# Early loads of a frequency-filter and mixer kernel reordered: filters behind the stage-1 stores, weights behind the low-rank loads, low-rank loads in three parts; stage 1 of units 2 and 3 moved later

## The chip, the cores and the metric

The kernel runs on one core of a Trainium2 chip. The metric is device time in microseconds (us), the median of several runs. Engines are named as in the profile: PE is TensorE (matmuls), PEld its weight loads, DVE VectorE, ACT ScalarE, POOL GpSimd, SP SyncE. SPq, ACTq and POOLq are DMA issues by these engines. Runs of one and the same kernel spread by 1 to 1.5%, so a difference needs an interval; each ratio below is given with its 95% interval.

One caution for all single traces: the profiled run of the kernel before had a granted PE clock of only 0.70 over its first 70 us. The other traces had 0.85 to 0.96 there, but for e17 (0.70), with the same program in many of them. Where a trace is compared with that of the kernel before in this stretch, the clock differs too.

## The reference, cut to what matters

```python
X = np.fft.rfft(x, axis=1)                  # x: 8 batches, 3136 tokens, 256 channels
y = np.fft.irfft(X * (filt_r + 1j * filt_i), n=3136, axis=1)
h = y.transpose(0, 2, 1) @ U @ V            # low rank, 32
u = y + h.transpose(0, 2, 1)
out = u + np.maximum(u @ w_ch1, 0) @ w_ch2  # 256 -> 1024 -> 256
```

## The kernel before: the parts that matter

3136 is 64 x 49. The transform is done in two steps with matmuls, and back. The eight batches are five units: two of one batch (units 0 and 1), three of two (units 2 to 4). For each unit:

- stage 1 (`f1`): x is loaded by POOL (in tiles x[0], x[1] and so on; the small rest is `xl`), transformed, evicted (copied out of the matmul's accumulators) to `asb` (the rest to `al`), and stored to the DRAM scratch `ct1` (shown as ct_0 to ct_4, one name for both scratches of a unit);
- stage 2 (`mid`): `a2` is loaded from it, 32 steps k multiply it with `tf2`, with the filters `fab` (DVE writes `uv`; for later units `fab` has a second half, filled by two mirror copies of 784 KB each just after the low rank of unit 0) and with `g3`; the result `esb` is stored to the scratch `ct2`;
- low rank: `eh` and `eb` are loaded from `ct2`, `ph` is accumulated, and DVE writes the rank-32 part into `eb` (`put_h`);
- mixer: `ut`, then `phh` (w1, relu `h`; its first matmul is called the first mm1), then `pc` (w2), then the output store `och`.

The mixer of unit n runs while stages 1 and 2 and low rank of unit n+1 are dealt out between its matmuls by a plan of steps. A step is about 1 us of mixer work. `S[n]` is the step at which the mixer of unit n starts.

```python
def hold(dst, src):                    # a 1x1 copy into the tile to be loaded:
    nc.vector.tensor_copy(dst, src)    # the load must wait for it, and it waits for src
...
    def third_loads(src):              # called at k == 10 of stage 2 of unit 0
        hold(usb[0:1, 0:1], src)
        nc.gpsimd.dma_start(usb, ...); nc.gpsimd.dma_start(vnat[64:96, :], moe_V)
        nc.gpsimd.dma_start(w1sb, ...); nc.gpsimd.dma_start(w2sb, ...)
    def fourth_loads(src):             # called when the low-rank loads of unit 0 land
        for c in range(4):
            load_x(units[1], c, src)
...
    deal(f1s[1], 7, 4, 11)             # stage 1 of unit 1: seven calls, steps 4 to 11
    deal(mids[1], 33, 17, 33)
    deal_f1(units[2], 12, (0, 2, 6, 7))
    deal(mids[2], 33, 44, S[2] - 29)
...
    # in the main loop, five steps before stage 1 of unit 2: its first two x loads,
    # held until x[2] of unit 1 has landed
    load_x(x_step[step], c, units[1].x[2][0:1, 0, 0:1] if x_step[step].n == 2 else None)
```

## Time and profile before

635.51 us, median of the first three runs (630.59 to 636.77). The profiled run spans 629.3 us.

The page of the kernel before, first its busy times, then its slices. A digit is tenths of a slice of 15.7 us; PEclk is the granted clock of PE, DMA the mean share of the 16 DMA engines.

```profile
span 629.3 us, 10769 instructions
PE 552.8 (88%) x4350; PEld 388.0 (62%) x4350; DVE 330.0 (52%) x390; ACT 334.6 (53%) x623; POOL 41.7 (7%) x62
...
PE   3294576999699993989999999999999999999997
...
PEclk9558576999979997989999999999999999999999
DMA  9898979999835749868567787455433862331112
```

PE is full in nearly the whole second half. It is idle for 76.5 us (629.3 minus 552.8), nearly all of it in the first 280 us, and 4.6 us at the end.

The chain that ended last, of the kernel before; columns are start, length and what.

```profile
9.72 7.16 DMA ct_0<-asb
16.96 6.25 DMA ct_0<-al
23.25 4.47 DMA a_161<-ct_0
28.58 10.14 DMA g_78<-g
...
69.42 13.53 DMA x<-in_x_dram
...
94.31 3.48 ACTq L320
99.42 3.85 ACTq L320
...
159.70 9.85 DMA eh<-ct_1
...
230.67 10.60 DMA ct_3<-asb
241.27 7.31 DMA eh<-ct_2
```

The early chain goes from transfer to transfer. Two of its pieces were the targets of the change: the stores of stage 1 at 10 to 23 us, and the loads and stores around the low rank of unit 2.

The timeline of the kernel before around 83 us; the bracket is the idle time before the instruction and what ended it.

```profile
83.05 0.14 DVE L174 COPY x<-x 1x1 f16<-1x1 f16 x1 [9.28 <-DMA x<-in_x_dram]
83.12 1.20 DVE L539 CAST ut<-pu 128x1024 f16<-128x1024 f32 x1
83.74 0.57 POOL L167 DMA_DIRECT2D x<-in_x_dram  x1 [12.32 <-DVE x L174]
84.38 1.01 PE L304 MATMUL pf<-x,wf_64 128*128 128x512 f16 x2 [3.87 <-DVE ut L539]
```

The first line is the hold for x of unit 2. It stands in the VectorE queue until x[2] of unit 1 lands at 83 us. The eviction of `ut` stands behind it, and PE stands 3.9 us behind that.

### The profile page before, as it was taken

The numbers are of one execution on the slowest core, as the hardware profiler recorded it, in microseconds if no ns is written. First come the engines' busy times: TensorE is split into PE (matmuls) and PEld (weight loads), VectorE is DVE, ScalarE is ACT, GpSimd is POOL, SyncE is SP. The second block draws the span as 40 slices with busy tenths as digits, with TensorE's granted clock in tenths as the row PEclk, the third lists the DMA queues.
The fourth block names the chain that finished last, engine by engine and source line by source line (L and its number), as shares of the span: only waits on it lengthen the run. The fifth ranks groups of instructions, "written<-read, shape, count | busy, mean of one in ns | idle before, by whom it ended". The sixth has DMA issues, their size and how long they took to land.

```text
span 629.3 us, 10769 instructions
## 1 busy us (share of the span) xinstructions
PE 552.8 (88%) x4350; PEld 388.0 (62%) x4350; DVE 330.0 (52%) x390; ACT 334.6 (53%) x623; POOL 41.7 (7%) x62
## 2 busy tenths in 40 slices
PE   3294576999699993989999999999999999999997
PEld 0183242767456661657766676777677767777776
DVE  5274222786278870263888743576866325333332
ACT  0043232667156662546667665665766655666663
POOL 3345110100000000000000000000000000000000
PEclk9558576999979997989999999999999999999999
DMA  9898979999835749868567787455433862331112
GB/s 176 230 205 193 214 183 236 246 250 244 244 119 161 216 81 286 208 166 227 171 187 173 208 245 249 156 148 187 120 131 119 239 202 83 99 100 67 66 67 102
DMA packets 68002, 110.18 MB, mean 175 GB/s; under 512 B 5549, under 2 KB 49438, under 8 KB 66604
## 3 DMA queue, kind: packets, MB, share of 16 engines
q1 hardware_dynamic: 36240, 81.17, 41.2%
q0 software_dynamic: 7312, 15.91, 15.8%
q10 hardware_dynamic: 24400, 12.41, 6.9%
q8 instruction: 34, 0.56, 0.4%
q14 instruction: 16, 0.13, 0.1%
HBM read 72.38 MB, written 51.38 MB: 197 GB/s over the span
## 4 chain that ended last, share of the span: by engine, by line
PE 73%; DMA 16%; issue 4%; DVE 3%; ACT 2%; ACTq 1%; POOL 0%; SPq 0%; POOLq 0%; DVEq 0%
PE phh L550 25%; PE pc L590 24%; PE pe L360 8%; PE pz L382 5%; PE pu L532 3%; PE pc L564 3%; DMA x<-in_x_dram 3%; PE pf L304 3%; DMA ct_3<-asb 2%; DMA g_78<-g 2%; DMA eh<-ct_1 2%; ACTq L320 1%; DMA eh<-ct_2 1%; DMA ct_0<-asb 1%; PE ph L476 1%
## 5 line engine op out<-in xcount | busy, mean ns | idle before, releaser
L550 PE MATMUL phh<-ut,w1sb 128*128 128x512 f16 (+2 forms) x848 | 251.7, 377 | 3.5 <-DVE ut L539 3.0
L397 DVE TENSOR_TENSOR uv<-pz,fab 98x1024 f16<-98x1024 f32 (+1 forms) x128 | 137.8, 1087 | 35.3 <-PE pz L382 34.8
L600 DVE COPY och<-pc 128x512 f32<-128x512 f32 x96 | 66.3, 690 | 165.8 <-PE pc L564 162.6
L550 PEld LDWEIGHTS <-w1sb 128*128 128x128 f16 x848 | 105.6, 146 | 36.7 <-issue 16.7
L366 ACT CAST esb<-pe 98x512 f16<-98x512 f32 (+1 forms) x160 | 79.5, 501 | 64.6 <-PE pe L360 57.0
L360 PE MATMUL pe<-uv,g_78 98*98 98x512 f16 (+1 forms) x320 | 85.7, 353 | 1.4 <-DMA g_78<-g 0.8
L539 DVE CAST ut<-pu 128x1024 f16<-128x1024 f32 (+1 forms) x51 | 59.9, 1174 | 21.6 <-PE pu L532 21.4
L564 PE MATMUL pc<-idn,ut 128*128 128x128 f16 x394 | 54.8, 220 | 0.0
L360 PEld LDWEIGHTS <-g_78 98*98 98x98 f16 x320 | 41.3, 132 | 19.4 <-issue 5.6
L564 PEld LDWEIGHTS <-ut 128*128 128x128 f16 x394 | 38.7, 98 | 6.7 <-issue 0.3
L382 PEld LDWEIGHTS <-tf_74 98*98 98x98 f16 x160 | 21.7, 136 | 20.2 <-DMA a_163<-ct_0 15.3
L304 PE MATMUL pf<-x,wf_64 128*128 128x512 f16 x84 | 27.9, 402 | 6.8 <-DVE ut L539 6.3
L476 PE MATMUL ph<-eh,ut_94 128*32 128x512 f16 (+1 forms) x120 | 10.7, 384 | 26.2 <-DMA eh<-ct_0 11.6
L167 POOL DMA_DIRECT2D x<-in_x_dram x24 | 14.1, 602 | 266.5 <-PE pf L304 225.1
L309 DVE CAST asb<-pf 128x1024 f16<-128x1024 f32 x21 | 25.6, 1219 | 11.5 <-PE pf L304 8.9
L307 ACT CAST asb<-pf 128x1024 f16<-128x1024 f32 x21 | 21.3, 1013 | 10.7 <-PE pf L304 6.7
L390 DVE TENSOR_TENSOR uv<-pz,fab 98x512 f16<-98x512 f32 x32 | 20.9, 687 | 5.1 <-PE pz L387 2.9
L476 PEld LDWEIGHTS <-ut_94 128*32 128x32 f16 x120 | 3.3, 97 | 31.6 <-issue 20.7
L366 ACT ACT_TABLE_LOAD x1 | 1.3, 1283 | 30.2 <-DVE uv L390 30.2
L382 PE MATMUL pz<-a_161,tf_74 98*98 98x256 f16 x8 | 3.2, 403 | 15.2 <-DMA a_163<-ct_0 14.9
L532 PEld LDWEIGHTS <-eb_97 96*128 96x128 f16 x256 | 10.3, 100 | 7.5 <-issue 4.7
L486 ACT CAST hp<-ph 128x512 f16<-128x512 f32 (+1 forms) x5 | 2.5, 501 | 23.1 <-PE ph L483 23.1
(1427 smaller groups left out, 1046.2 us busy)
## 6 DMA issues: line engine op xcount, KB each, us to landing
out_dram<-och SPq DMA_DIRECT2D x48, 512.0 KB
x<-in_x_dram POOLq DMA_DIRECT2D x24, 512.0 KB, 8.0
ct_2<-esb SPq DMA_DIRECT2D x16, 196.0 KB
ct_3<-esb SPq DMA_DIRECT2D x16, 196.0 KB
ct_4<-esb SPq DMA_DIRECT2D x16, 196.0 KB
ct_2<-asb ACTq DMA_DIRECT2D x6, 512.0 KB
ct_3<-asb ACTq DMA_DIRECT2D x6, 512.0 KB
eh<-ct_2 SPq DMA_DIRECT2D x6, 512.0 KB
```

The source lines that it names most:

```text
L304: nc.tensor.matmul(pf[:, i, :], wx, u.x[c][:, r:r + 2, :], start=True, stop=True)
L309: nc.vector.tensor_copy(dst, pf)
L360: nc.tensor.matmul(pe[0:98, 0:bd], g3[:, (2 * k + l) * 98:(2 * k + l + 1) * 98], uv[:, l * bd:(l + 1) * bd], start=(l == 0), stop=(l == 1))
L366: nc.scalar.copy(st["esb"][:, i, :], pe[0:98, 0:bd])
L382: nc.tensor.matmul(pz[0:98, 0:bd], wz, a2[c][:, i, :], start=True, stop=True)
L397: nc.vector.tensor_mul(uv.rearrange("p (f b d) -> p f b d", f=2, b=nb), zin, fin)
L532: nc.tensor.matmul(pu[:, dh, 64 * i:64 * i + 64], e2[0:96, d0:d0 + 128], sv[0:96, 64 * r:64 * r + 64], start=(i == 0), stop=True, skip_gro ...
L539: nc.vector.tensor_copy(gr.ut[:, :, 0:n].rearrange("p h (c q s) -> p h c q s", q=64, s=2), pu[:, :, 0:n].rearrange("p h (c s q) -> p h c q ...
L550: nc.tensor.matmul(ph[:, 0:n], w1v[:, dh, :, t], gr.ut[:, dh, 0:n], start=(dh == 0), stop=(dh == 1))
L564: nc.tensor.matmul(o[:, dh * 128:dh * 128 + 128], gr.ut[:, dh, t0:t0 + n], idn, start=False, stop=(dh == 1), skip_group_check=True)
L590: nc.tensor.matmul(o, gr.h[tt][:, i * 128:(i + 1) * 128], w2sb[:, tt * DM:(tt + 1) * DM], start=(tt == 0), stop=False, skip_group_check=True)
L600: nc.vector.tensor_copy(dst, gr.pc.rearrange("p (j d) -> p j d", j=2))
```

## The change

Its intent: let the stage-1 stores of unit 0, and later its low-rank loads, have the DMA engines to themselves, by moving loads that are wanted later; and keep stage 1 of units 2 and 3 away from the loads of the units ahead. The diff, cut to its core:

```diff
-    load_filters(PARTS[0], PARTS[1])                 # was right behind x of unit 0
+    def first_loads(src):                            # src: the last stage-1 eviction
+        hold(tf2[0:1, 0:1], src);  nc.sync.dma_start(tf2[:, 0:...], ...)
+        hold(g3[0:1, 0:1], src);   nc.scalar.dma_start(g3[:, 0:2 * KA], ...)
+        load_part(0, tf2[:, 0:1])                    # filters wait for tf2 to land
     def second_loads(src):                           # a2[0] has landed
-        for i in range(2, 4):
-            load_part(i, src)
+        load_part(1, src)                            # parts 2 and 3 at k == 1 and k == 6
     def third_loads(src):
-        nc.gpsimd.dma_start(w1sb, ...); nc.gpsimd.dma_start(w2sb, ...)
     def fourth_loads(src):
+        hold(w1sb[96:97, 0:1], src);  nc.gpsimd.dma_start(w1sb, ...)
+        hold(w2sb[96:97, 0:1], src);  nc.gpsimd.dma_start(w2sb, ...)
         for c in range(4):
             load_x(units[1], c, src)
@@ stage 1 of unit 0
-                        nc.vector.tensor_copy(dst[:, i, :], pf)
+                        (nc.scalar.copy if i else nc.vector.tensor_copy)(dst[:, i, :], pf)
@@ low rank of unit 0: rows 0 to 31, 32 to 63 -> 0 to 31, 32 to 47, 48 to 63
-            a = 32
+            for z in (32, 48):
...
-        if i == 24:                                  # i counts k of stage 2 of unit 0
+        if i in (22, 29):
             next(ranks[0])
@@ plan
-    deal(f1s[1], 7, 4, 11);  deal(mids[1], 33, 17, 33)
-    deal_f1(units[2], 12, ...);  deal(mids[2], 33, 44, S[2] - 29)
+    deal(f1s[1], 7, 5, 12);  deal(mids[1], 33, 18, 34)
+    deal_f1(units[2], 20, ...);  deal(mids[2], 33, 53, S[2] - 26)
-    deal_rank(units[1], 34, S[1] - 7);  deal_rank(units[2], S[2] - 28, S[2] - 7)
+    deal_rank(units[1], 35, S[1] - 6);  deal_rank(units[2], S[2] - 25, S[2] - 6)
@@ unit 3 (and one step of unit 4's low rank)
-        stage 1 from S[2] - 38, stage 2 from S[2] + 21 to S[3] - 36, low rank S[3] - 35 to S[3] - 8
+        stage 1 from S[2] - 18, stage 2 from S[2] + 40 to S[3] - 30, low rank S[3] - 29 to S[3] - 7
```

More of the change, by code (lines that the diff above doesn't have):

```diff
@@ L222, in load_part @@
     def load_part(i, src):
-        hold(fab[0:1, 0, PARTS[i], 0:1], src)
-        load_filters(PARTS[i], PARTS[i + 1])
+        a, z = PARTS[i], PARTS[i + 1]
+        hold(fab[:, 0, a, 0:1], src)
+        if z == NK:
+            hold(fab[:, 0, 31, 0:1], src)
+        load_filters(a, z)
+    def first_loads(src):
+        hold(tf2[0:1, 0:1], src)
+        nc.sync.dma_start(tf2[:, 0:PARTS[1] * 147], tf2_d[:, 0:PARTS[1] * 147])
+        hold(g3[0:1, 0:1], src)
+        nc.scalar.dma_start(g3[:, 0:2 * KA], g_d[:, 0:2 * KA])
+        load_part(0, tf2[:, 0:1])
     def second_loads(src):
-        for i in range(2, 4):
-            load_part(i, src)
+        load_part(1, src)
         for t, d in ((s2, s2_d), (s2t, s2t_d), (kr, kr_d)):
-            hold(t[0:1, 0:1], src)
+            hold(t[0:1, 0:1], src[0:1])
             nc.scalar.dma_start(t, d)
         ka = PARTS[1] * 147
-        hold(tf2[0:1, ka:ka + 1], src)
+        hold(tf2[0:1, ka:ka + 1], src[0:1])
         nc.sync.dma_start(tf2[:, ka:], tf2_d[:, ka:])
-        hold(g3[0:1, 2 * KA:2 * KA + 1], src)
+        hold(g3[0:1, 2 * KA:2 * KA + 1], src[0:1])
         nc.sync.dma_start(g3[:, 2 * KA:], g_d[:, 2 * KA:])
@@ L241, in third_loads, with fourth_loads @@
         nc.gpsimd.dma_start(vnat[64:96, :], moe_V)
+    def fourth_loads(src):
+        hold(w1sb[96:97, 0:1], src)
         nc.gpsimd.dma_start(w1sb, moe_w_ch1.rearrange("(h dd) c -> dd h c", h=2))
+        hold(w2sb[96:97, 0:1], src)
         nc.gpsimd.dma_start(w2sb, moe_w_ch2.rearrange("(cc t) e -> cc (t e)", t=8))
-    def fourth_loads(src):
         for c in range(4):
@@ L309, in f1 @@
                         nc.vector.tensor_copy(dst, pf)
-                if u.n == 0:
-                    if (c, half) == (1, 0):
-                        hold(tf2[0:1, 0:1], asb[0:1, 0, 0:1])
-                        nc.sync.dma_start(tf2[:, 0:PARTS[1] * 147], tf2_d[:, 0:PARTS[1] * 147])
-                    if (c, half) == (2, 0):
-                        hold(g3[0:1, 0:1], asb[0:1, 0, 0:1])
-                        nc.scalar.dma_start(g3[:, 0:2 * KA], g_d[:, 0:2 * KA])
                 if half and nb == 1:
@@ L331, in f1 @@
         al = sb.tile([m, DM], F16, tag="al", bufs=1)
-        if u.n == 0:
-            nc.vector.tensor_copy(al, pf[0:m, 0, 0:DM])
-            load_part(1, al[0:1, 0:1])
-        else:
-            nc.scalar.copy(al, pf[0:m, 0, 0:DM])
+        nc.scalar.copy(al, pf[0:m, 0, 0:DM])
         (nc.sync if u.n == 0 else nc.scalar).dma_start(
             dram(u.ct1, 48 * 64 * bd, [[DM, m], [1, DM]]), al)
+        if u.n == 0:
+            first_loads(al[0:1, 0:1])
         yield
@@ L374, in mid @@
         if u.n == 0:
-            second_loads(a2[0][0:1, 0, 0:1])
+            second_loads(a2[0][:, 0, 0:1])
         for k in range(NK):
@@ L397, in mid @@
                 nc.vector.tensor_mul(uv.rearrange("p (f b d) -> p f b d", f=2, b=nb), zin, fin)
+            if u.n == 0 and k in (1, 6):
+                load_part(2 if k == 1 else 3, uv[:, 0:1])
             if u.n == 0 and k == 10:
@@ L457, in low_rank @@
         if u.n == 0:
-            a = 32
-            for c in range(3):
-                load(c, 0, a)
-            load_l(0, a)
-            yield
+            for z in (32, 48):
+                for c in range(3):
+                    load(c, a, z)
+                load_l(a, z)
+                a = z
+                yield
         for c in range(3):
@@ L466, in low_rank @@
         load_l(a)
-        u.held = eh[2]
+        u.held = eh[1]
         u.ready = True
@@ L628 @@
             next(sr)
-        if i == 24:
+        if i in (22, 29):
             next(ranks[0])
-        if i == 28:
+        if i == 25:
             u_hat()
@@ L634 @@
     next(ranks[0])
-    fourth_loads(units[0].held[64:65, 0, 0:1])
+    fourth_loads(units[0].held[96:97, 0, 0:1])
     for _ in range(3):
@@ L659, in deal_f1 @@
             k += 1
-    deal(f1s[1], 7, 4, 11)
-    deal(mids[1], 33, 17, 33)
-    deal_f1(units[2], 12, (0, 2, 6, 7))
-    deal(mids[2], 33, 44, S[2] - 29)
+    deal(f1s[1], 7, 5, 12)
+    deal(mids[1], 33, 18, 34)
+    deal_f1(units[2], 20, (0, 2, 6, 7))
+    deal(mids[2], 33, 53, S[2] - 26)
     def deal_rank(u, a, z):
@@ L672, in deal_rank @@
         plan[step_at(z + 2)].append(ranks[u.n])
-    deal_rank(units[1], 34, S[1] - 7)
-    deal_rank(units[2], S[2] - 28, S[2] - 7)
+    deal_rank(units[1], 35, S[1] - 6)
+    deal_rank(units[2], S[2] - 25, S[2] - 6)
     for u in units[3:]:
-        deal_f1(u, S[u.n - 1] - (38 if u.n == 3 else 60), (1, 7))
-        deal(mids[u.n], 33, S[u.n - 1] + (21 if u.n == 3 else 3), S[u.n] - 36)
-        deal_rank(u, S[u.n] - 35, S[u.n] - 8)
+        deal_f1(u, S[u.n - 1] - (18 if u.n == 3 else 60), (1, 7))
+        deal(mids[u.n], 33, S[u.n - 1] + (40 if u.n == 3 else 3), S[u.n] - (30 if u.n == 3 else 36))
+        deal_rank(u, S[u.n] - (29 if u.n == 3 else 35), S[u.n] - 7)
     x_step = {max(0, next(i for i, p in enumerate(plan) if f1s[u.n] in p) - 5): u for u in units[2:]}
```

## The prediction

> **What bounds it now.** The page gives PE 552.8 us busy of 629.3 (88%). The table by stretches shows PE full from about 280 to 600 us; the change removes no PE work, so only idle time and lost clock can be won. The 76 us of PE idle lie at 0-30 us (23), 50-70 (13), 70-90 (6), 90-110 (6), 160-200 (7), 240-280 (11) and the end (5). In the first 140 us the DMA share is 0.7 to 1.1 in every 10 us, at about 216 GB/s: the start is bound by transfers, and PE is granted only 0.5 to 0.7 of its clock in much of it. The chain of waits names the ct_0 stores (7.2 us), the al store behind them (6.3), the a2 load (4.5), the g3 remainder (10.1), the low-rank loads, x of unit 1 (13.5), stage-1 stores of unit 1 (ACT blocked 3.5 and 3.9 us), later eh<-ct_1 (9.9) and, after ct_3<-asb (10.6), eh<-ct_2 (7.3; PE waits 10.5 us at 238-248).
>
> **What the change does.** It moves bytes and removes none. (a) 0-28 us: filter parts 0 and 1, tf2 and g3 (about 1.3 MB landed) no longer share the engines with 1.6 MB of stage-1 stores; ACT takes half of the evictions (0.68 us each on DVE, about 1 us won). Estimate: first uv at 25 to 26 us instead of 28.5; filter part 0 now waits for tf2 to land, which caps the gain. (b) w1 and w2 (1 MB landed, 7.5 and 9.9 us) leave 45-55 us, so the last esb stores (issued 55.5, landed 61.6) and the low-rank loads should land sooner, but w1 is then wanted some 8 us after its issue. Estimate: first mm1 at 66 us instead of 73.2. (c) A DVE hold for x of unit 2 waits for x[2] of unit 1 until 83.05 and blocks the ut eviction behind it: PE idle 3.9 us. Eight steps later it should find its data there. Unit 2's x and stores also leave the 84-110 us where ACT was blocked. Estimate: 5 to 7 us. (d) Stage 1 of unit 3 leaves the low-rank loads of unit 2 alone: most of the 10.5 us wait and part of the slow clock after it (0.83 in 240-280). Estimate: 8 us. (e) The eh<-ct_1 wait near 165 us: 1 to 2 us at most; stage 1 of unit 2 now overlaps it more.
>
> The Trainium skill, "DMA: Bandwidth & Descriptors" (Queues, rings and completion order), says each DMA engine goes round-robin between the queues with work; so a load issued early takes its share from the stores of the moment. The 6.3 us for a 32 KB store agree.
>
> **Prediction.** Sum of the estimates about 7 + 6 + 8 + 2 = 23 us, nearly all on the chain: 612 us, range 600 to 625. Chances: faster by over 2% 0.80, within 2% 0.18, slower by over 2% 0.02.
>
> **What would show each step.** First uv before 27 us, al store under 4 us (a). First mm1 near 66 us; if w1 releases it, (b) is partly given back. No long DVE hold near 80, ACT issues under 2 us at 85-100, stage 2 of unit 1 starting before 103 instead of 113.6 (c). PE wait for eh<-ct_2 under 4 us (d). PE idle near 58 us.
>
> **What would make it wrong.** Filter part 1 or the rest of tf2 or g3 arriving after their k; w1 late; x of unit 1, now behind 1 MB of weights in the same queue, late for step 5; stage 2 of unit 2 packed so densely (33 calls over 19 steps instead of 25) that its stores are late for its low-rank loads, moving the wait rather than removing it.

## The result, and the profile after

The changed kernel takes 664.45 us (median of 4 runs, 661.32 to 666.57) against 633.05 us for the kernel before (4 runs, 628.87 to 636.77). The ratio is 1.0494, 95% interval 1.0406 to 1.0582: slower by 5%. A ratio here is the mean time of one kernel's runs over that of the other's of the same rounds, so it is not quite the ratio of the medians quoted. Executions over 1.5% slower than the fastest of the same kernel are left out of the means.

The page of the changed kernel, the same lines (a slice is 16.5 us):

```profile
span 659.5 us, 10783 instructions
PE 555.9 (84%) x4350; PEld 385.6 (58%) x4350; DVE 325.4 (49%) x387; ACT 338.8 (51%) x630; POOL 41.7 (6%) x62
...
PE   3066436799679999639999999899999999999997
...
PEclk9998588699979999959999999999999999999999
DMA  7977878679975535957787827953552662332112
```

PE has the same work and is idle 103.6 us (659.5 minus 555.9) instead of 76.5. So 27 of the 30 us between the two profiled runs are idle PE. The DMA engines, too, are less busy at the start than before (a share of 0.83 in the first 60 us, against 0.94).

The chain that ended last, of the changed kernel:

```profile
17.20 5.47 DMA tf_74<-tf
...
24.91 12.97 DMA fab<-in_filt_i_dram
...
67.75 2.88 DMA eh<-ct_0
71.13 0.49 POOL w1sb L254
73.42 27.32 DMA x<-in_x_dram
...
115.18 9.37 DMA ct_1<-al
...
170.40 8.64 DMA ct_1<-esb
179.09 3.84 DMA eh<-ct_1
...
268.20 18.44 DMA ct_3<-asb
286.70 3.06 DMA out_dram<-och
```

The stage-1 stores of unit 0 are off the chain, as intended. In their place stand the filters (13 us), and x of unit 1 takes 27 us instead of 13.5.

The lines that answer to those at 83 us, in the timeline of the changed kernel:

```profile
100.83 0.14 DVE L174 COPY x<-x 1x1 f16<-1x1 f16 x1 [15.43 <-DMA x<-in_x_dram]
100.90 1.20 DVE L320 CAST asb<-pf 128x1024 f16<-128x1024 f32 x1
101.52 0.57 POOL L167 DMA_DIRECT2D x<-in_x_dram  x1 [26.06 <-DVE x L174]
102.16 1.01 PE L315 MATMUL pf<-x,wf_64 128*128 128x512 f16 x2 [12.17 <-DVE asb L320]
```

The hold was to be harmless after the move of stage 1 of unit 2. It is not: in the built program it still stands ahead of the stage-1 evictions of unit 1 on VectorE, and x[2], which it waits for, lands 18 us later. PE stands 12.2 us.

The end of that wait, in the table by stretches of the changed kernel; the last three figures are PEclk, DMA share and GB/s:

```profile
90.00:95.00 5.00, 0.00 (x0) 0.00 (x0) 0.00 (x0) 0.29 (x1) 0.00 (x0) 1.00 0.48 160
95.00:100.00 5.00, 0.00 (x0) 0.00 (x0) 0.00 (x0) 0.00 (x0) 0.00 (x0) 0.50 0.43 113
```

A share of 0.43 to 0.48 does not mean engines that wait for work. Counted packet by packet from 91.5 to 99 us, never fewer than seven packets are in flight, and at 71% of the moments exactly seven (7 of 16 is 0.44). They are mostly 16 KB packets of the mirror copies, whose queue has at most seven in flight, and 4 KB packets of x in another queue. This reads as seven engines full and nine empty, with the last packets of x among those of the mirror copies, which were issued at 77 to 79 us. No run splits the mirror copies in the changed kernel, so their part of the delay is not measured.

To compare many runs, I cut each at the starts of the low-rank writes (`put_h`) of units 0 to 4. The table gives the length of each segment and, in brackets, PE's idle time in it (length minus PE busy, from the table by stretches).

| profiled run | to unit 0 | to unit 1 | to unit 2 | to unit 3 | to unit 4 | to the end |
|---|---|---|---|---|---|---|
| before | 70.0 (37.6) | 102.3 (18.0) | 95.1 (13.1) | 129.8 (3.2) | 121.4 (0.0) | 110.6 (4.6) |
| changed | 73.4 (42.8) | 116.5 (31.7) | 101.3 (17.0) | 135.9 (6.4) | 122.2 (0.7) | 110.2 (5.0) |

The largest single loss is 14 us between the low ranks of units 0 and 1, but every segment up to unit 3 loses. One caution about such tables: two of the programs below (e6 and e11) are the same on PE through this segment, and their traces show 101.2 and 106.5 us in it. Differences of 5 us there, between single traces, prove nothing alone (nor do 4 us before it: e4 has the early loads of the changed kernel, and its first `put_h` is at 69.4 us, not 73.4).

### The profile page after: what moved, and what is told of

It reads as the page before. It is cut to its first block, busy times and chain, and to the rows that moved or that the text cites. A ratio compares the mean times of both kernels' runs of the same rounds, so it can differ in the third digit from the quotient of the medians.

```text
span 659.5 us, 10783 instructions
## 1 busy us (share of the span) xinstructions
PE 555.9 (84%) x4350; PEld 385.6 (58%) x4350; DVE 325.4 (49%) x387; ACT 338.8 (51%) x630; POOL 41.7 (6%) x62
## 4 chain that ended last, share of the span: by engine, by line
PE 66%; DMA 22%; DVE 5%; ACT 3%; issue 2%; SPq 1%; POOL 1%; ACTq 0%; DVEq 0%; POOLq 0%
PE phh L555 22%; PE pc L595 20%; PE pe L362 8%; PE pz L384 6%; DMA x<-in_x_dram 5%; DMA ct_3<-asb 3%; PE pc L569 3%; PE pf L315 3%; PE pu L537 3%; DMA ct_4<-asb 2%; DMA fab<-in_filt_i_dram 2%; DMA ct_1<-al 1%; ACT esb L368 1%; DMA ct_1<-esb 1%; DVE ut L544 1%
## 5 line engine op out<-in xcount | busy, mean ns | idle before, releaser
L555 PEld LDWEIGHTS <-w1sb 128*128 128x128 f16 x848 | 105.4, 146 | 37.2 <-issue 13.5
L362 PE MATMUL pe<-uv,g_78 98*98 98x512 f16 (+1 forms) x320 | 82.6, 341 | 0.8 <-ACT esb L368 0.6
L362 PEld LDWEIGHTS <-g_78 98*98 98x98 f16 x320 | 39.0, 127 | 18.4 <-issue 5.3
L315 PE MATMUL pf<-x,wf_64 128*128 128x512 f16 x84 | 27.5, 395 | 15.7 <-DVE asb L320 12.6
L481 PE MATMUL ph<-eh,ut_90 128*32 128x512 f16 (+1 forms) x120 | 10.9, 394 | 29.3 <-DMA eh<-ct_2 10.7
L384 PEld LDWEIGHTS <-tf_74 98*98 98x98 f16 x160 | 20.8, 130 | 14.9 <-issue 11.0
L392 DVE TENSOR_TENSOR uv<-pz,fab 98x512 f16<-98x512 f32 x32 | 20.0, 676 | 13.5 <-DMA fab<-in_filt_i_dram 12.0
L481 PEld LDWEIGHTS <-ut_90 128*32 128x32 f16 x120 | 3.1, 98 | 34.1 <-issue 22.3
L315 PEld LDWEIGHTS <-wf_64 128*128 128x128 f16 x84 | 7.5, 100 | 20.8 <-issue 16.8
L537 PE MATMUL pu<-sv,eb_91 96*128 96x64 f16 x256 | 12.3, 199 | 5.9 <-DVE eb_91 L425 5.9
```

Source lines behind the costliest of these rows:

```text
L315: nc.tensor.matmul(pf[:, i, :], wx, u.x[c][:, r:r + 2, :], start=True, stop=True)
L362: nc.tensor.matmul(pe[0:98, 0:bd], g3[:, (2 * k + l) * 98:(2 * k + l + 1) * 98], uv[:, l * bd:(l + 1) * bd], start=(l == 0), stop=(l == 1))
L384: nc.tensor.matmul(pz[0:98, 0:bd], wz, a2[c][:, i, :], start=True, stop=True)
L537: nc.tensor.matmul(pu[:, dh, 64 * i:64 * i + 64], e2[0:96, d0:d0 + 128], sv[0:96, 64 * r:64 * r + 64], start=(i == 0), stop=True, skip_gro ...
L555: nc.tensor.matmul(ph[:, 0:n], w1v[:, dh, :, t], gr.ut[:, dh, 0:n], start=(dh == 0), stop=(dh == 1))
```

## The experiments

Theory A: the early reorder loses the time, because it puts 1 MB of weights in front of x of unit 1. Rival B: the moved schedule of units 2 and 3 loses it.

### e1, the early loads alone

The changed kernel with all plan lines as before.

> The changed kernel with the schedule of stages 1, 2 and low rank of units 1 to 4 put back as before; only the reordered early loads remain. Theory A (the early loads lose the time: first filters late, weights in front of x of unit 1, a VectorE hold on that x): first mm1 near 79 us again, x[2] of unit 1 near 100 us, and 15 to 30 us slower than the kernel before (648 to 663 us). Rival B (the moved schedule of units 2 and 3 loses it): within 1% of the kernel before, 627 to 640 us.

645.29 us against 632.3; ratio 1.0204 (1.0136 to 1.0272). The hold is released at 100.1 us, first mm1 is at 77.4 us. The time lies between the two forecasts. The early half costs 2.0%, some two fifths of the loss, and A holds for that part alone. Cut as above, e1 takes 116.6 us (30.0) to unit 1, like the changed kernel, and 93.4 (12.7) and 130.3 (3.6) to units 2 and 3, like the kernel before.

### e2, the schedule alone

The kernel before with all plan lines as changed.

> The kernel before with only the schedule of units 1 to 4 moved as in the change. Theory A: early stage as before (mm1 at 73 us, x[2] at 83 us), total between 610 and 635 us, because the low-rank loads of unit 2 lose their competition. Rival B: 650 us or more.

649.9 us; ratio 1.0257 (1.0189 to 1.0324). The schedule, which I had counted as a gain, costs 2.6%. 649.9 lies just under the rival's 650, and far from theory A's 610 to 635. Both halves lose, and 2.0% and 2.6% make up the 4.9% of the whole to within their intervals.

### e3, weights back, all else as changed

```diff
     def third_loads(src):
+        nc.gpsimd.dma_start(w1sb, ...); nc.gpsimd.dma_start(w2sb, ...)
     def fourth_loads(src):
-        hold(w1sb[96:97, 0:1], src);  nc.gpsimd.dma_start(w1sb, ...)
-        hold(w2sb[96:97, 0:1], src);  nc.gpsimd.dma_start(w2sb, ...)
```

> The changed kernel with w1 and w2 put back behind U and V (issued during stage 2 of unit 0); all else as changed. If the weights in front of x of unit 1 cause the 12 us stop of PE near 90-101 us and the 3.6 us wait for w1: x[2] lands near 88 us, mm1 at 75 to 76 us, total 642 to 652 us. If x is late for another reason (the mirror copies, eb loads): still near 660 us.

655.38 us (651.51 to 658.29); ratio 1.0343 (1.0267 to 1.0418), while the changed kernel had 661.32 to 666.57. x[2] lands at 90.9 us instead of 100.8, a little later than the 88 expected. The median lies above the 642 to 652 forecast, and its interval just touches that of the changed kernel. First mm1 was at 78.2 us: it did not come earlier. But `put_h` of this trace came 1.6 us later than in the changed kernel (75.0 against 73.4), so the trace doesn't show whether the 3.6 us wait for w1 cost anything.

### e4, the hold on GpSimd

```diff
-    hold(t[0:1, 0:1], after)
+    (eng or nc.vector).tensor_copy(t[0:1, 0:1], after)   # eng = nc.gpsimd for this one hold
```

> The changed kernel with one instruction moved: the 1x1 copy that makes the first x loads of unit 2 wait for x[2] of unit 1 runs on GpSimd, which issues those loads, instead of VectorE. Nothing else waits less. If the VectorE hold is what stops PE for 12 us: PE idle at 90-101 us falls to 3 us or less and the total to 650 to 655 us. If stage 1 of unit 1 waits for x[2] anyway: total within 3 us of the changed kernel, 660 to 666 us.

660.61 us (656.47 to 662.23); ratio 1.0423 (1.0352 to 1.0494). Some 4 us of medians below the changed kernel, with overlapping intervals, and not the 10 expected. With the hold gone from VectorE, PE waits 7.8 us for x itself. The hold spreads the wait for x to VectorE; it is not its cause.

### e5 and e6, the schedule in two parts

e5 is the kernel before with the plan lines of units 1 and 2, e6 with those of units 3 and 4.

> The kernel before with only the schedule lines of units 1 and 2 moved (stage 1 of unit 2 from step 12 to 20, stage 2 and low rank of units 1 and 2 later); units 3 and 4 as before. Theory C: stage 1 of unit 2 now lies on the last ct_1 store and the low-rank loads of unit 1, and low rank of unit 2 has less lead; then this part alone costs 8 to 14 of the 17 us, with the last ct_1<-esb store taking 7 us or more (3.3 before). Rival D (the loss is in the lines of units 3 and 4): within 4 us of the kernel before.

> The kernel before with only the schedule lines of units 3 and 4 moved (stage 1 of unit 3 twenty steps later, stage 2 19 steps later, its low rank with 6 steps less lead). Theory C: 3 to 8 us slower, from a wait for the low-rank loads of unit 3 near 400 us (5 us in the schedule-only run), and no loss before 300 us. Rival D: 12 us or more slower. My prediction's step (d) would have it 8 us faster, by emptying the wait for eh<-ct_2 at 238-248 us.

| run | median | ratio (95%) | to unit 1 | to unit 2 | to unit 3 |
|---|---|---|---|---|---|
| e5 | 635.9 | 1.0072 (0.9989 to 1.0154) | 105.5 (22.2) | 96.8 (11.1) | 128.3 (4.9) |
| e6 (3 runs) | 633.3 | 1.0036 (0.9952 to 1.0120) | 101.2 (18.6) | 91.8 (10.9) | 136.6 (6.5) |
| e2 (both) | 649.9 | 1.0257 (1.0189 to 1.0324) | 107.0 (22.3) | 100.2 (17.1) | 137.6 (8.9) |

Neither part alone is surely slower (0.7 and 0.4%), and together they cost 2.6%. e6 is the closest test of my step (d). Its low rank of unit 2 does come 3.3 us sooner, but idle PE falls there by only 2.2 us; the rest is PE work that no longer lies before this mark. At unit 3 idle PE grows by 3.3 us. There the last low-rank loads now come on the chain:

```profile
380.99 9.29 DMA eh<-ct
```

In the kernel before no wait of PE for `eh<-ct_3` shows in this stretch. The move did not empty a wait; it passed it on.

The e5 expectation of a late last store of unit 1 is seen: the chain of e5 has

```profile
156.01 8.62 DMA ct<-esb
164.71 4.02 DMA eh<-ct
```

The matching store of the kernel before is issued at 155.15 us, and its low-rank loads follow at 158.43 us. Loads and stores of stage 1 of unit 2 now lie on it. But the eh loads that follow are shorter (4.0 instead of 9.9 us), so only part of this is lost.

### e7, e8 and e9, the early reorder in three parts

Each is the kernel before with one part: e7 the filters, tf2 and g3 with the split evictions; e8 the weights; e9 the low-rank loads in three parts.

> The kernel before with only the first part of the early reorder (filters behind the stage-1 stores and behind tf2, in steps; half of the stage-1 evictions on ScalarE); weights, low-rank loads and schedule as before. If the late first filters (38.0 us instead of 28.5) cost what stage 2 of unit 0 shows at its end: first uv at 36 to 38 us, first mm1 2 to 4 us late, total 2 to 5 us slower. If stage 2 of unit 0 makes it all good by running without waits: within 1 us of the kernel before.

631.8 us (3 runs) against 631.95; ratio 1.0003 (0.9916 to 1.0090). First uv is at 39.2 us, ten later than before, and yet nothing is lost at the end. Stage 2 of unit 0 catches up: from first uv to the last `esb` eviction it takes 22.6 us (39.20 to 61.77), against 27.0 us (28.53 to 55.55) before, and from there to `put_h` 10.9 us against 14.5. That its loads had landed by then is one reason that I can think of. The clock is another: it was 1.00 from 25 to 62 us in e7 and 0.68 in the trace of the kernel before. With the same early loads as before and clocks of 0.83 to 0.94, the traces of e6, e10, e11, e12, e14 and e16 take 24.2 to 28.5 us. So a catching up of 1.6 to 5.9 us is left at clocks nearer to that of e7; what brings it about is not shown.

> The kernel before with only w1 and w2 moved behind the low-rank loads, in front of x of unit 1. If the weights in front of x cost it: first mm1 waits for w1 by 2 to 4 us or not at all (low rank ends earlier), x[2] of unit 1 lands 8 to 12 us later than 83 us, total 5 to 10 us slower. If the early part gains as much as the late part loses: within 3 us of the kernel before.

639.5 us; ratio 1.0121 (1.0049 to 1.0194): the weights alone cost 1.2%. The table by stretches shows what was vacated. First the kernel before, then e8; after the stretch and the busy times of the engines come PEclk, DMA share and GB/s at the end of each line. A share can come out a little over 1.

```profile
50.00:55.00 5.00, 4.39 (x30) 2.93 (x28) 3.66 (x6) 3.06 (x10) 4.88 (x1) 1.00 1.08 223
```

```profile
50.00:55.00 5.00, 4.39 (x30) 2.98 (x29) 4.07 (x7) 3.10 (x10) 3.26 (x1) 1.00 0.30 76
```

The engines fall to 0.30 busy at 50 to 55 us, and PE does exactly what it did (4.39 us in both). The second part of the low-rank loads is issued at 61.68 us, as before (61.62). So the weights had been in the way of neither. In their new place they are: x of unit 1, behind them in the same POOL queue, is issued at 69.68 us and lets the hold go only at 96.72 us, 27 us later; before it took 14.7 us (68.37 to 83.05).

> The kernel before with only the low-rank loads of unit 0 in three parts (rows 0 to 31, 32 to 47, 48 to 63) instead of two, as in the change. Theory: in the changed kernel the last esb store stands in the in-order SP queue behind the second part, which waits for the store ahead of it; so the last store is issued 5 to 6 us late (64.7 us), and what the smaller last part gains is spent: first mm1 within 2 us of 73.2 us or up to 4 us later, total 0 to 6 us slower. Rival: the early reorder loses its 13 us in the weights alone (7.7 us measured) and this part is free: within 2 us of before.

638.88 us; ratio 1.0096 (1.0019 to 1.0172). Filters, weights and parts, 0.0, 1.2 and 1.0%, add up to the 2.0% of e1 to within their intervals. The SP timeline of e9:

```profile
61.38 1.87 SPq L448 DMA_DIRECT2D eh<-ct  x3
63.29 0.58 SPq L453 DMA_DIRECT2D e2l<-ct  x1
63.98 0.35 SPq L368 DMA_DIRECT2D ct<-esb  x1
66.68 1.81 SPq L448 DMA_DIRECT2D eh<-ct  x3
```

The last esb tile was ready at 56.67 us. Its store stands behind the second part of the low-rank loads, which waits on SP for an earlier store, and goes out at 63.98 us. The Trainium skill, "DMA: Bandwidth & Descriptors" (Anatomy of one DMA), says that a semaphore wait happens on the issuing sequencer before dispatch; this trace agrees, with 7.3 us for a store that had nothing left to wait for. Even so, `put_h` comes only 1.7 us later, counted from the last esb tile (16.2 us instead of 14.5). The rest of the loss comes behind it: x[2] lands 20.7 us after issue instead of 14.7. Why x is slower there, I did not find; from 86 to 92 us about seven packets are in flight there too, mostly of the mirror copies.

### e10 to e12, attempts at something faster

e10 is the kernel before with the e4 edit. e11 is the kernel before with stage 1 of unit 3 moved as in the change, but with the end of its stage 2 (`S[3] - 36`) and its low-rank window as before. e12 is both.

> The kernel before with the wait of the first x loads of unit 2 moved from VectorE to GpSimd. My prediction's step (c) said that this hold stops PE for 3.9 us near 80-84 us. If so, 2 to 4 us faster. If stage 1 of unit 1 waits for x[2] itself a moment later: within 1 us.

629.07 us against 631.4; ratio 0.9953 (0.9882 to 1.0024). Not shown to be faster. Its timeline shows why the 3.9 us stop is not simply won:

```profile
85.26 1.01 ACT L307 CAST asb<-pf 128x1024 f16<-128x1024 f32 x1 [2.09 <-PE pf L304]
86.30 12.60 ACTq L320 DMA_DIRECT2D ct<-asb  x2
99.00 1.01 ACT L307 CAST asb<-pf 128x1024 f16<-128x1024 f32 x1 [12.23 <-issue]
```

Stage 1 of unit 1 starts 5 us sooner, and then ACT spends 12.6 us on issuing two stores. Stage 2 of unit 1 starts at 112.6 us instead of 113.6.

> The kernel before with stage 1 of unit 3 twenty steps later and its stage 2 from step 40, but with the end of its stage 2 and its low-rank lead as before (35 steps, 8 at the end). If the loss of the unit-3 lines lies in the shorter lead (29 steps), the wait near 380-400 us (3 to 5 us in the unit-3 run) is gone and the wait of low rank of unit 2 is 2 us smaller: total 0 to 4 us faster than before. If it lies in the denser packing: no better than the unit-3 run, 2 to 3 us slower than before.

638.54 us; ratio 1.0104 (1.0040 to 1.0168). With the lead restored, the move of stage 1 of unit 3 still loses, and it is not better than e6 (their intervals overlap). So the lead alone is not its cost. Here 33 calls of stage 2 lie in 22 steps instead of 41. How the loss divides between packing and what else, these runs don't tell.

> Both of the two last edits on the kernel before. If they are independent their gains add: 2 to 7 us faster than before (626 to 630 us). If one of them is worth nothing: as the other alone.

635.09 us; ratio 1.0053 (0.9990 to 1.0115). No gain in the sum.

### e13 to e15, three inferences tested

> The kernel before with the low-rank loads of unit 0 in three parts, but the second part (rows 32 to 47) issued on GpSimd's queue, so that nothing stands in front of the last esb store on SP. If the cost of the three parts (6 us) is the last store held up behind the second part: the last store is issued near 56 us instead of 64, first mm1 at 71 to 74 us, total within 3 us of before or faster. If the three parts cost for another reason (more, smaller transfers): again 5 to 8 us slower.

```diff
-                    load(c, a, z);  load_l(a, z)
+                    load(c, a, z, nc.gpsimd if z == 48 else nc.sync);  load_l(a, z, ...)
```

635.3 us against 630.9; ratio 1.0055 (1.0000 to 1.0110). Within the first theory's band, but this interval overlaps that of e9, so the times don't separate the two. The trace does show the store freed: the last tile is ready at 52.81 us, and the last group of stores is on its way by then.

```profile
49.47 3.68 SPq L368 DMA_DIRECT2D ct<-esb  x3
58.95 1.86 SPq L448 DMA_DIRECT2D eh<-ct  x3
```

`put_h` of unit 0 starts at 66.3 us, 3.7 us before the kernel before (2.7 of it because stage 2 happened to end sooner). And all of it is gone at the start of stage 2 of unit 1: 113.2 us.

> The schedule-only run with the end of stage 2 and the low-rank window of unit 2 put back (end S2-29, low rank S2-28 to S2-7, instead of S2-26, S2-25 to S2-6). If the shorter lead of unit 2's low rank makes the parts cost more together than apart: PE idle between the low-rank ends of units 1 and 2 falls from 17 to about 11 us, total 636 to 643 us. If not: 646 to 652 us as the schedule-only run.

643.76 us; ratio 1.0204 (1.0161 to 1.0246). Idle PE on the way to unit 2 falls from 17.1 to 11.6 us, as expected of the shorter lead. The time falls from 1.0257 to 1.0204 only, with overlapping intervals, and just misses the 636 to 643. So the lead may explain a part of what the two schedule parts cost together; the times don't show it, and the rest is open.

> The kernel before with the unit-2 hold on GpSimd (as in e10) and x of unit 1 waiting for the first part of the low-rank loads (near 55-57 us) instead of the second (67.9 us): bytes moved out of the saturated 68-96 us into 57-65 us, where the DMA share falls to 0.5. If bytes in the saturated stretch are what counts: x[2] lands near 75 us, stage 1 of unit 1 ends 3 to 8 us earlier, total 2 to 6 us faster than before (625 to 629 us). If x then delays the last stores and low-rank loads as much as it gains: within 2 us of e10 (629 us).

639.67 us; ratio 1.0128 (1.0084 to 1.0173): slower, against both expectations. x is issued at 59.2 us, but the edit moved more than bytes. The holds of x of unit 1 are VectorE copies, and they now stand in front of the last `uv` of stage 2 of unit 0:

```profile
58.76 0.27 DVE L166 COPY x<-eh 1x1 f16<-1x1 f16 x3 [6.16 <-DMA eh<-ct]
59.06 0.69 DVE L390 TENSOR_TENSOR uv<-pz,fab 98x512 f16<-98x512 f32 x1
59.81 0.66 PE L360 MATMUL pe<-uv,g 98*98 98x256 f16 x2 [5.31 <-DVE xl L174]
```

They wait for the first low-rank loads, and the last `uv` and PE wait with them. The last esb tile is ready at 60.88 us instead of 55.55. The SP timeline shows the second low-rank part issued at 70.85 us instead of 61.62:

```profile
53.41 7.81 SPq L368 DMA_DIRECT2D ct<-esb  x3
70.85 1.80 SPq L448 DMA_DIRECT2D eh<-ct  x3
```

Those loads wait for the esb stores. `put_h` of unit 0 comes at 81.2 us, 11 us late, and 5.3 of the 11 us are the hold's. From the last tile to the second low-rank part it then takes 10.0 us instead of 6.1, with x in flight beside the last store. That fits the mechanism that I had wanted the weights to show, a load that takes its share from a store of the moment, but no run shows it without the hold.

### e16 to e18, bytes taken out of the stretch

The two mirror copies of the filters, 784 KB each at 74 us, in four parts; the later three at steps 14, 17 and 20 of the plan. e17 adds the hold on GpSimd, e18 also the e13 edit.

```diff
-    mirror_filters(0, NK)
+    mirror_filters(0, 8)
+    # in the plan: hold on the mixer's ut, then mirror_filters(a, a + 8), a in (8, 16, 24)
+    deal(mirrors, 3, 14, 23)
```

> The kernel before with the two mirror copies of the filters (784 KB each, issued at 74 us) in four parts: the first quarter as before, the others at steps 14, 17 and 20, while stage 2 of unit 1 runs and before it needs them. If bytes between 68 and 112 us set the start of stage 2 of unit 1: x[2] of unit 1 lands 3 to 5 us earlier, stage 2 of unit 1 starts 3 to 6 us before 113.6 us, total 3 to 6 us faster. If that start hangs on latency (stores, then reads) and not on bytes, or the moved bytes delay it there: within 2 us of before.

> The last edit and the unit-2 hold on GpSimd (e10, 2 to 3 us faster alone). If both take different waits away: 5 to 9 us faster than before (622 to 626 us). If the bytes are not the limit: 2 to 3 us faster, as e10.

> The last run with the low-rank loads of unit 0 in three parts, the second on GpSimd's queue (e13: low rank ends 3.7 us earlier in its trace, all given back before stage 2 of unit 1). If the transfer-bound stretch swallowed that gain, it now stays: 2 to 4 us faster than e17. If not: within 2 us of e17 or slower.

633.68, 630.1 and 630.68 us against 629.61; ratios 1.0049 (0.9995 to 1.0103), 0.9999 (0.9950 to 1.0048) and 1.0027 (0.9964 to 1.0090). No gain anywhere. x[2] of e16 lands at 79.8 us, 3 us earlier, but ACT then spends 9.3 us on two store issues (from 88.29 us), and stage 2 of unit 1 starts at 112.3 us. The expectation that fewer bytes before it would start it earlier fell. (The second quarter of the copies went out at 81 us already, so less was moved away than I had meant.) No version here beats the kernel before.

What can be said of this stretch is in one table, each row one trace. x[2] is the landing of the last full x tile of unit 1, read from the release of the hold.

| run | x[2] of unit 1 | stage 2 of unit 1 starts |
|---|---|---|
| e16 | 79.8 | 112.3 |
| e10 | 82.4 | 112.6 |
| before | 83.1 | 113.6 |
| e13 | 85.0 | 113.2 |
| e7 | 85.8 | 116.3 |
| e3 | 90.9 | 123.0 |
| e9 | 91.3 | 122.9 |
| e8 | 96.7 | 123.2 |
| e1 | 100.1 | 130.0 |
| changed | 100.8 | 128.7 |

Up to about 85 us the start stays at 112 to 114 us (111.7 in e17, 115.5 in e2); in the traces of e10 and e16 an earlier x is given back in blocked store issues on ACT. Beyond that the start is later where x is later. e15 is not in the table: its x[2] lands at 69.7 us, but `put_h` is 11 us late, and stage 2 of unit 1 starts at 119.7. So the change had much to lose here and hardly anything to win. What sets the floor at 112 us I could not settle.

## Why the prediction was wrong

The prediction was 612 us, faster, with a 2% chance of over 2% slower. It measured 664. Two steps of the sum failed, (b) and (c) with (d), so that 23 us won became 30 us lost. Step (b) held that the weights at 45 to 55 us delay the last stores and the low-rank loads. They did not (loads issued at 61.68 us without them, 61.62 with them), and in their new place they delayed x of unit 1 by 12 us from issue to landing (27.0 against 14.7 in e8, which costs 1.2%). Steps (c) and (d) held that a later stage 1 of units 2 and 3 empties waits. The moved schedule alone costs 2.6% (e2): the wait for `eh<-ct_2` stayed (10.7 us in the changed kernel instead of 10.5), and in the trace of e2 idle PE grew on the way to each of units 1 to 3 (22.3, 17.1 and 8.9 us instead of 18.0, 13.1 and 3.2). How that loss divides inside the schedule stays open. Point by point:

- **Bounds.** Right: only idle PE changed. Busy PE moved from 552.8 to 555.9 us, idle from 76.5 to 103.6 (58 predicted).
- **(a) "first uv at 25 to 26 us".** This step failed too, but cheaply. The stores did land sooner: a2 was issued at 21.3 us instead of 23.3, and the first matmul of stage 2 ran at 25.60 us. (From the issue of the al store to that of a2 it took 5.3 us, more than the 4 us that I had named.) But uv waited 12 us more for the filters, to 38.0 us. The size varies from trace to trace: with the same early loads, first uv came at 31.4 us in e1 and at 34.4 in e4. I had named the wait for tf2 as a cap and had not sized it: the filters were issued at 23 to 25 us, into the a2 loads and the remainders of tf2 and g3. It cost little: e7, this part alone, is within 0.9% of before either way.
- **(b) "the last esb stores and the low-rank loads should land sooner".** This step failed. It took a full DMA share for proof that the weights delay what runs beside them. e8 emptied 50 to 55 us to a share of 0.30, and the low-rank loads were issued at 61.68 instead of 61.62 us. I used the skill's page to say that a load issued early takes its share from the stores of the moment; that needs stores in flight at that moment. e15, where x meets the last store, fits that, but half of its delay is a hold's, so the sharing is not shown by itself.
- **(b) again, the queue.** I listed "x of unit 1, now behind 1 MB of weights in the same queue" as a risk, and gave it no time. It was one of the two costs of the early part: x[2] at 100.8 us, PE stopped 12.2 us. The other, the low-rank loads in three parts (1.0%, e9), my prediction did not price at all. In the last 10 us of that wait the DMA share was near 0.45, which reads as seven full engines that x shared with the mirror copies.
- **(c) "eight steps later it should find its data there".** Wrong twice. The hold did not stand later relative to the stage-1 evictions of unit 1 on VectorE, and its data came 18 us later. Without the hold (e4, e10), PE waits for x itself or ACT for its store issues: worth 0.5%, not shown, rather than 5 to 7 us.
- **(d) "most of the 10.5 us wait" for eh<-ct_2.** Wrong. The changed kernel waits 10.7 us for it in four pieces, and DVE 13.0 us for an output store issued behind these loads. e6 alone won 2.2 us of idle PE there and lost 3.3 at the next unit; both schedule parts together cost 2.6%. I took the transfers of unit 3 away from one low rank without asking which low rank they go to, and how much lead each has left.
- **(e)** The last ct_1 store took 8.6 us instead of 3.3, and PE's wait for eh<-ct_1 rose from 4.1 to 6.8 us, where I expected 1 to 2 us won.
- **What would make it wrong.** Three items of that list came true (w1 late by 3.6 us, x late, dense packing moving the wait), and a fourth nearly (the filters, but at the first k). I gave a loss of over 2% a chance of 2%, since each item looked small alone.

Shown: early loads 2.0%, of which weights 1.2 and three parts 1.0, filters none; schedule 2.6%. Its two parts alone measured 0.7 and 0.4%, neither clear of zero. Open: why the schedule parts seem to cost more together (the lead of unit 2 may be a part), why x is slower in the three-part runs, and what keeps stage 2 of unit 1 from starting before 112 us.

## What to carry to other kernels

Before you move a load out of a busy stretch, find the instruction that ends up waiting there and ask whether its transfer is in flight at the same time; a full DMA share is not a wait, and a share of 0.45 can be seven full engines with your load among them. Then ask the same of the place where the load goes, first of the queue it joins: everything behind it on that queue can be late (x[2] by 13.7 us behind 1 MB of weights in e8), and a wait in an in-order queue (a hold on VectorE, a load on SP) is passed on to ready work behind it. In a schedule where each unit hides behind the last, moving one unit later takes the lead from its own next stage, so count the idle time at the next two marks, not at the one you meant to improve.

## What the Trainium skill lacked or had wrong

- "DMA: Bandwidth & Descriptors" (Issuing engines are not separate DMA queues) says that issuing from several engines saves only sequencer time, "usually small relative to the DMA itself". Here it was not small: two store issues held ACT for 12.6 us in e10 and 9.3 us in e16 (86 to 99 us), with ready evictions behind them. No section that I found tells how long such an issue can be held, or how many transfers a queue takes before it is.
- The same page (Anatomy of one DMA) puts the semaphore wait on the issuing sequencer. It could say what that does to ready work: a ready store stood 7.3 us behind a waiting load on SP in e9.
- "TensorE: Matmul & The Clock Gate" (Part 1) describes a clock halved after idle windows. The trace agrees: 0.50 in 60 to 65 us with PE idle, 1.00 in the full stretches. The page lacked nothing here. The changed kernel had the higher mean clock in its profiled run (0.945 against 0.926; other runs of the kernel before reach 0.958) and was slower: idle time, not the clock, decided.
